# Dealing 32 weight-decode steps out anew among eight experts, with their raw words loaded one call earlier

## The chip, the cores and the metric

One core of one Trainium2 chip. The metric is the device time of one execution in microseconds (us). Engines: PE does matmuls (PEld loads its weights), DVE the vector work, ACT activations and copies, POOL index work and indirect DMAs, SP issues the other DMAs. Each engine works through its own queue in order.

## The reference

Three layers, each feeding the next. In float32:

```python
# 1. attention over 576 positions, 4 batches, 8 heads of 64; a causal window of 128; a bias per head
attn = softmax(where(mask, scale * q @ k.T + bias, -1e9)) ; x = attn @ v        # -> [2304, 512]
# 2. mixture of 8 experts: each token goes to the one with the largest logit
e = argmax(x @ w_gate); g = softmax(x @ w_gate)[e]
x = g * (relu(x @ w1[e]) @ w2[e])                                                # w1 [8,512,1024], w2 [8,1024,512]
# 3. one wide layer
out = relu(x @ w_in) ** 2 @ w_out                                                # w_in [512,2048], w_out [2048,512]
```

The weights of the third layer (w_in and w_out) arrive as 64-bit floats, so the kernel reads them as pairs of 32-bit words and makes 32-bit floats of them itself.

## The kernel before

Products are made from float16 pairs: a matrix is split into a high part (ACT: a cast with a scale) and a low part (DVE: what the cast left over), and three matmuls with float32 accumulation stand for one product. Only the first expert's product with w1 is done in float32.

**Order of the stages.** Attention comes first, and tokens are given to experts as it goes. The experts follow in an order found at run time (by how many tokens they have); the places in that order have fixed row counts (`ROWS`, 384 down to 224). Place e has two products: `s1` (8 column blocks `fc`, `h = relu(x w1)`; L790 to L792 on PE, L793 on ACT, L794 on DVE) and `s2` (4 blocks `d`; L844 to L846 on PE, a copy to `yT` on ACT, L847). While place e is computed, the weights of place e + 1 are brought in: after every second `fc` a quarter of w1, after every `d` a quarter of w2 (`load_w`). Each quarter is a DMA of 512 KB into a staging buffer (L742), split by ACT (L764) and DVE (L765) into a ring of 12 float16 tiles. The rest, tokens that found no room, is done under a branch (`overflow`, L1053) that is normally not taken, and the wide layer comes last (`moe2`).

**The decode steps.** The wide layer's weights must be ready, decoded and split, when that layer begins. This is cut into 32 steps that are strewn among the experts: 8 output steps (`out_step`, a block of w_out that is stored to DRAM again, `SENT`), 16 input steps (`in_step`, a piece of w_in, with four sums and differences of its blocks, since the wide input product has seven block products instead of eight, and hence seven operands), and 8 more output steps (`KEPT`). A step is: DMA of the raw words (one of 512 KB or two of 256 KB, L859), three word operations on DVE that make a float of a 64-bit pair (L864 to L866), for an input step four adds (L887 to L890), and a finish: the cast on ACT (L895 or L911) and the remainder on DVE (L896 or L912). All steps decode into one tile, `dec`.

**Where they are called.** `wide()` (L920) does one call: it finishes the step of the call before, then takes the next step, issues its DMAs and its decode. `STEPS` holds for each place at which `fc` of `s1` and after which `d` of `s2` a call stands. Counted from the code, calls lie thus: 6 ahead of place 0, then 2, 3, 2, 3, 3, 3, 3, 6 in the places 0 to 7, and 3 behind the branch. The seventh place (6) also starts the normalisation of the next layer.

**Buffers.** Raw words and weight quarters share four staging buffers (tag `rw`, bufs 4). Besides, the tiles `wi4` to `wi7`, which hold finished input weights later, serve as staging for part of the weights until they are needed: `SPARE` names which for each place, and `stage` (L748) takes them for every second quarter (every one for place 1).

**What sets the order.** The kernel is written for a framework that places the waits and decides each engine's order at build time: what stands earlier in the code goes first, but an instruction that is expected to be ready may go ahead of an earlier one that isn't. The order is fixed when the program runs.

Of the kernel before, what the change touches and what calls it, by code (L numbers as in the profile page):

```python
# [10 lines left out]
F32 = mybir.dt.float32  # L11
# [11 lines left out]
N, DM, E, F, F2 = 2304, 512, 8, 1024, 2048  # L23
# [22 lines left out]
TINY, HUGE = 1e-30, 1e30  # L46
GT = 2
GW = GT * P
STEPS = (((2, 6), ()), ((1, 5), (1,)), ((4,), (1,)), ((1, 5), (1,)), ((1, 5), (1,)), ((3,), (1, 3)), ((3,), (1, 3)),
         ((1, 3, 5, 7), (1, 3)))  # L50
SPARE = ((), (4, 5, 6, 7), (4, 5, 6, 7), (4, 5, 6, 7), (4, 5, 6, 7), (6, 7), (7,), ())
KEPT = (0, 1, 8, 9, 2, 3, 10, 11)
SENT = (4, 5, 12, 13, 6, 7, 14, 15)

# [35 lines left out]
class K:  # L90
# [656 lines left out]

    def stage(self, which, e, c):  # L748

        free = SPARE[e]  # L750
        n = 4 * (which - 1) + c
        if n % 2 == 0 and e > 1 or not free or (which, e) == (1, 1):
            return self.raw()
        return self.wi_s[free[(n if e == 1 else n // 2) % len(free)]].rearrange("p k a c -> p (k a c)").bitcast(F32)[:, :1024]

# [59 lines left out]
    def part(self, byte, n, dt=F32):  # L815
        t = self.work[:, byte // 4:byte // 4 + n * (2 if dt != F32 else 4) // 4]
        return t if dt == F32 else t.bitcast(dt)
# [33 lines left out]
    def wide_load(self, src, pieces):  # L851
        nc, V = self.nc, self.nc.vector
        n = sum(w for _, _, w, _ in pieces)
        wide = src.dtype != F32
        st = self.raw(U32 if wide else F32)[:, :1024 if wide else 512]
        for rows, c0, w, dst in pieces:
            r = src.bitcast(U32)[rows] if wide else src[rows]
            k = 2 if wide else 1
            nc.sync.dma_start(dst(st, k), c0(r, k))  # L859
        if not wide:  # L860
            return st
        t = self.dec[:, 512:] if len(pieces) > 1 else self.dec[:, :512]
        w = st.rearrange("p (n a) -> p n a", a=2)
        V.tensor_scalar(t, w[:, :, 1], 3, 0x3FFFFFFF, op0=ALU.logical_shift_left, op1=ALU.bitwise_and)  # L864
        V.scalar_tensor_tensor(t, w[:, :, 1], 0xC0000000, t, op0=ALU.bitwise_and, op1=ALU.bitwise_or)  # L865
        V.scalar_tensor_tensor(t, w[:, :, 0], 29, t, op0=ALU.logical_shift_right, op1=ALU.bitwise_or)  # L866
        return t.bitcast(F32)

    def in_step(self, fp, kp):

        nc, V = self.nc, self.nc.vector

        def part(j):
            blocks = slice(0, 4, 3) if j == 0 else slice(1, 3)
            return (slice((2 * j + kp) * P, (2 * j + kp + 1) * P),
                    lambda r, k: r.rearrange("p (i c) -> p i c", i=2)[:, :, k * fp * P:k * (fp + 1) * P],
                    2 * P,
                    lambda st, k: st.rearrange("p (b c) -> p b c", b=4)[:, blocks])

        f = self.wide_load(self.wi, [part(0), part(1)])  # L880
        d = self.dec.bitcast(F32).rearrange("p (b c) -> p b c", b=8)
        f4 = f.rearrange("p (b c) -> p b c", b=4)
        if self.wi.dtype == F32:
            nc.vector.tensor_copy(d[:, 4:], f4)
        a11, a12, a22, a21 = (d[:, 4 + b] for b in range(4))
        s1, s2, s3, s4 = (d[:, b] for b in range(4))
        V.tensor_tensor(s1, a21, a22, op=ALU.add)  # L887
        V.tensor_tensor(s3, a11, a21, op=ALU.subtract)
        V.tensor_tensor(s2, s1, a11, op=ALU.subtract)
        V.tensor_tensor(s4, a12, s2, op=ALU.subtract)  # L890
        src = self.dec.bitcast(F32)[:, :7 * P]
        dst = self.wi_s[fp]

        def finish():
            nc.scalar.activation(dst[:, kp, 0], src, AF.Copy, scale=WISC)  # L895
            nc.vector.scalar_tensor_tensor(dst[:, kp, 1], src, WISC, dst[:, kp, 0], op0=ALU.mult, op1=ALU.subtract)  # L896

        return finish

    def out_step(self, fc):  # L900

        nc = self.nc
        f = self.wide_load(self.wo, [(slice(fc * P, (fc + 1) * P), lambda r, k: r, DM, lambda st, k: st)])

        def finish():
            if fc in KEPT:
# [8 lines left out]
                self.stored.append(lambda: nc.sync.dma_start(self.wod[:, o:o + 2 * DM],  # L915
                                                             dst.rearrange("p a d -> p (a d)")))

        return finish

    def wide(self, k=1):  # L920
        def store():
            while len(self.stored) > (2 if self.steps and self.steps[0][0] != self.in_step else 0):
                self.stored.pop(0)()

        for _ in range(k):
            store()
            if self.finish:
                self.finish()
                self.finish = None
            if self.steps:  # L930
                f, *a = self.steps.pop(0)
                self.finish = f(*a)

    def open_wide(self, stack):
        wp = self.wp = stack.enter_context(self.tc.tile_pool(name="wp", bufs=1))
        self.wi_s = [wp.tile([P, 2, 2, 7 * P], F16, name=f"wi{k}", tag=f"wi{k}") for k in range(8)]
        self.wo_s = {}
        self.stored, self.finish = [], None
        self.steps = [(self.out_step, fc) for fc in SENT] + \
            [(self.in_step, fp, kp) for fp in range(8) for kp in range(2)] + [(self.out_step, fc) for fc in KEPT]  # L940

# [13 lines left out]
    def experts(self, stack):  # L955
# [35 lines left out]
        with tc.issue_after(self.last_gather.ins):  # L991
            for f in self.late:
                f()
        wide(2)
        self.s2([w[2, 0, k] for k in range(4)], self.hte, 0, EB * P, lambda d: wide())
        xt = self.new_xf(P)
        self.transpose_whole(xgs[0][0], xt)
# [226 lines left out]
    def moe2(self):  # L1224
# [9 lines left out]
        self.load_columns()  # L1234
        self.wide1(0, 1, first)
        self.turn_columns()
        while self.finish:
            self.wide()
        self.fetch_out()
        for G in range(NG):  # L1240
# [75 lines left out]
```

## Time and profile before

| | |
|---|---|
| median of three runs | 775.46 us (773.32, 775.46, 777.34) |
| profiled execution | 774.25 us, of which the span is 772.2 us |
| mean granted clock of TensorE | 0.984 of 2.4 GHz |
| busy share of the span | PE 94%, PEld 72%, DVE 70%, ACT 47%, POOL 17% |
| moved by DMA | 91.63 MB |

A profile shows one execution. The span runs from the first to the last instruction; what the execution takes beside it is outside the profile. The span is cut into stretches (windows), and for each the busy time of every engine is given, with the clock that TensorE was granted and the share in which the DMA engines were busy. An instruction's idle time before it is put down to what ended last among the things it waited for. An engine's queue is in order, so what waits at its head holds up all behind it.

In the profiled execution the experts begin at 179.93 us (first product of place 0) and the first matmuls of place 7 at 382.78; the branch is passed at about 415 us, and the wide layer takes the rest.

### The profile page before, as it was taken

To read this page: it belongs to the slowest core of one execution; us is meant where nothing else is said; L and a number is where in the kernel's file an instruction comes from. 1 tells how busy PE (TensorE), PEld (TensorE's weight loads), DVE (VectorE), ACT (ScalarE), POOL (GpSimd) and SP (SyncE) were. 2 spreads that over 40 slices of the span, in tenths; PEclk is the share of its full clock that TensorE was granted. 3 is DMA by queue.
4 is the path that set the end of the run, shared out by engine and by line. 5 is a ranking of instruction groups with operands and counts; after the bars stand their busy time and mean duration, and the time that the engine had idled before them with its cause. 6 is when DMAs were issued, how large, how long until landed. Compare 5 with 4: busy or idle time off the path is not lost. (4 is left out here: it accounts for less than half of the span.)

```text
span 772.2 us, 18404 instructions
## 1 busy us (share of the span) xinstructions
PE 728.1 (94%) x7547; PEld 559.2 (72%) x7547; DVE 540.1 (70%) x1352; ACT 361.2 (47%) x636; POOL 133.7 (17%) x183
## 2 busy tenths in 40 slices
PE   6989999998989899899798999999999999999996
PEld 5889899787646566688698777777777777777772
DVE  5898788855879897568798774747474756566440
ACT  5878898744556574465444342423232323323220
POOL 4583421525543020000000010101010000000001
PEclk9999999899999999999899999999999999999999
DMA  9796214867897874457514000000000000000000
GB/s 336 291 388 149 67 56 120 240 177 213 286 311 231 272 252 136 152 171 249 181 57 138 3 28 2 29 1 29 2 22 8 15 15 15 15 14 15 15 14 28
DMA packets 35650, 91.63 MB, mean 119 GB/s; under 512 B 5209, under 2 KB 13547, under 8 KB 35547
## 3 DMA queue, kind: packets, MB, share of 16 engines
q1 hardware_dynamic: 29803, 75.77, 30.3%
q0 software_dynamic: 5760, 14.65, 5.7%
q8 instruction: 61, 1.00, 0.5%
q14 instruction: 26, 0.21, 0.1%
HBM read 77.54 MB, written 13.04 MB: 117 GB/s over the span
## 5 line engine op out<-in xcount | busy, mean ns | idle before, releaser
L1159 PEld LDWEIGHTS <-wi 128*128 128x128 f16 x3024 | 170.4, 98 | 6.4 <-issue 2.6
L1220 POOL DMA_INDIRECT out_dram<-o,oid x18 | 17.5, 973 | 464.5 <-ACT o L1218 464.5
L1179 ACT CAST wr<-work 128x1024 f16<-128x1024 f32 x36 | 37.6, 1045 | 123.1 <-DVE work L1178 123.1
L845 PE MATMUL ps_c<-work,wr 128*128 128x352 f16 (+5 forms) x256 | 73.8, 294 | 10.2 <-DVE work L794 9.4
L844 PE MATMUL ps_c<-work,wr 128*128 128x352 f16 (+5 forms) x256 | 73.5, 293 | 5.9 <-ACT work L793 3.2
L846 PE MATMUL ps_c<-work,wr 128*128 128x352 f16 (+5 forms) x256 | 73.9, 294 | 0.0
L305 PE MATMUL ps_a<-yT,wr 128*128 128x192 f32 (+2 forms) x288 | 64.3, 343 | 6.6 <-DMA wr<-in_q_dram 5.0
L1184 DVE TENSOR_TENSOR work<-work 128x512 f32<-128x512 f32 x18 | 12.4, 692 | 77.2 <-ACT work L1171 77.2
L1159 PE MATMUL ps_c<-work,wi 128*128 128x128 f16 x1032 | 64.9, 219 | 0.0
L1159 PE MATMUL ps_a<-work,wi 128*128 128x128 f16 x1032 | 64.7, 219 | 0.0
L317 ACT ACTIVATE pb<-pb,nm 128x192 f32<-128x192 f32 (+2 forms) x144 | 56.2, 433 | 12.4 <-DVE nm L310 11.7
L1159 PE MATMUL ps_b<-work,wi 128*128 128x128 f16 x960 | 60.1, 219 | 1.5 <-DVEq L1057 1.5
L1211 PE MATMUL ps_d<-wr 128*128 128x512 f16 x144 | 54.6, 379 | 0.1
L1212 PE MATMUL ps_d<-wr 128*128 128x512 f16 x144 | 54.6, 379 | 0.0
L1213 PE MATMUL ps_d<-wr 128*128 128x512 f16 x144 | 54.6, 379 | 0.0
L1213 PE MATMUL ps_d<-rw,wr 128*128 128x512 f16 x144 | 54.6, 379 | 0.0
L1212 PE MATMUL ps_d<-rw,wr 128*128 128x512 f16 x144 | 54.6, 379 | 0.0
L1211 PE MATMUL ps_d<-rw,wr 128*128 128x512 f16 x144 | 54.6, 379 | 0.0
L1213 PEld LDWEIGHTS <-wr 128*128 128x128 f16 x288 | 28.1, 98 | 33.9
L765 DVE SCALAR_TENSOR_TENSOR wr<-rw,wr 128x1024 f16<-128x1024 f32 x36 | 43.7, 1217 | 11.1 <-ACT wr L764 11.0
L1180 DVE TENSOR_TENSOR wr<-work,wr 128x1024 f16<-128x1024 f32 x36 | 44.0, 1221 | 10.0 <-ACT wr L1179 10.0
L305 PEld LDWEIGHTS ps_a<-yT,wr 128*128 128x128 f32 x288 | 45.1, 199 | 7.8 <-DMA yT<-in_k_dram 6.1
(248 smaller groups left out, 1693.8 us busy)
## 6 DMA issues: line engine op xcount, KB each, us to landing
rw<-in_w_dram SPq DMA_DIRECT2D x36, 512.0 KB, 5.5
wi<-in_w_dram SPq DMA_DIRECT2D x24, 512.0 KB, 5.3
rw<-in_wo_dram SPq DMA_DIRECT2D x16, 512.0 KB, 4.2
rw<-in_wi_dram SPq DMA_DIRECT2D x32, 256.0 KB, 5.2
wr<-in_q_dram SPq DMA_DIRECT2D x14, 512.0 KB, 8.0
xd<-xhl POOLq DMA_DIRECT2D x16, 256.0 KB, 4.5
yT<-in_k_dram SPq DMA_DIRECT2D x7, 576.0 KB, 10.7
rw<-in_v_dram SPq DMA_DIRECT2D x12, 325.0 KB, 5.6
```

The costliest lines, as they stand in the source:

```text
L305: nc.tensor.matmul(ps[:, s, first:hi], q[g, u, hh // 4][:, hh % 4, s if u < 4 else 0, :], self.kt[g, hh // 2][:, hh % 2, key0:key0 + hi - ...
L317: self.last_exp = nc.scalar.activation(pb[:, s, first:hi], pb[:, s, first:hi], AF.Exp, bias=nm[:, s:s + 1], scale=-1.0)
L765: self.nc.vector.scalar_tensor_tensor(t[:, 1], st, sc, t[:, 0], op0=ALU.mult, op1=ALU.subtract)
L844: nc.tensor.matmul(py, wh, hh, start=fc == 0, stop=False)
L845: nc.tensor.matmul(py, wh, hl, start=False, stop=False)
L846: self.last_mm = nc.tensor.matmul(py, wl, hh, start=False, stop=fc == 7)
L1159: self.nc.tensor.matmul(ps[:, j], w[:, kp, a, w0 * P:(w0 + 1) * P], v[:, 2 * x + kp], start=kp + b == 0, stop=kp == 1 and b == 2)
L1179: nc.scalar.copy(g[0][:, :, i], ci)
L1180: V.tensor_tensor(g[1][:, :, i], ci, g[0][:, :, i], op=ALU.subtract)
L1211: nc.tensor.matmul(py, gh, wh, start=n == 0, stop=False)
L1212: nc.tensor.matmul(py, gh, wl, start=False, stop=False)
L1213: nc.tensor.matmul(py, gl, wh, start=False, stop=n == 15)
```

## The change

`STEPS` deals the calls out anew: 7 ahead of place 0, then 3, 4, 3, 4, 3, 1, 0, 6 in the places 0 to 7, and 3 behind the branch. A step is now a generator with three parts, and each call of `wide()` begins one step and moves every begun step on by one part, the oldest first: so a call finishes the step begun two calls earlier, decodes the one begun in the call before, and issues the DMAs of a new one. `SPARE` goes; `stage` counts how many input steps have begun and offers as staging those of `wi4` to `wi7` whose own step is at least two steps off, for every second quarter as before (from place 2 on). In `moe2` the loop that drains the steps asks for `begun`.

```diff
--- before.py
+++ after.py
@@ -46,9 +46,8 @@
 TINY, HUGE = 1e-30, 1e30
 GT = 2
 GW = GT * P
-STEPS = (((2, 6), ()), ((1, 5), (1,)), ((4,), (1,)), ((1, 5), (1,)), ((1, 5), (1,)), ((3,), (1, 3)), ((3,), (1, 3)),
+STEPS = (((1, 4, 6), ()), ((1, 5), (0, 2)), ((5,), (0, 2)), ((1, 5), (0, 2)), ((3,), (0, 2)), ((), (1,)), ((), ()),
          ((1, 3, 5, 7), (1, 3)))
-SPARE = ((), (4, 5, 6, 7), (4, 5, 6, 7), (4, 5, 6, 7), (4, 5, 6, 7), (6, 7), (7,), ())
 KEPT = (0, 1, 8, 9, 2, 3, 10, 11)
 SENT = (4, 5, 12, 13, 6, 7, 14, 15)
 
@@ -747,9 +746,10 @@
 
     def stage(self, which, e, c):
 
-        free = SPARE[e]
+        begun = 16 - sum(f == self.in_step for f, *_ in self.steps) if e > 0 and (which, e) != (1, 1) else 16
+        free = [k for k in range(4, 8) if begun + 2 <= 2 * k]
         n = 4 * (which - 1) + c
-        if n % 2 == 0 and e > 1 or not free or (which, e) == (1, 1):
+        if n % 2 == 0 and e > 1 or not free:
             return self.raw()
         return self.wi_s[free[(n if e == 1 else n // 2) % len(free)]].rearrange("p k a c -> p (k a c)").bitcast(F32)[:, :1024]
 
@@ -857,7 +857,11 @@
             r = src.bitcast(U32)[rows] if wide else src[rows]
             k = 2 if wide else 1
             nc.sync.dma_start(dst(st, k), c0(r, k))
-        if not wide:
+        return st
+
+    def wide_words(self, st, pieces):
+        nc, V = self.nc, self.nc.vector
+        if st.dtype == F32:
             return st
         t = self.dec[:, 512:] if len(pieces) > 1 else self.dec[:, :512]
         w = st.rearrange("p (n a) -> p n a", a=2)
@@ -877,7 +881,10 @@
                     2 * P,
                     lambda st, k: st.rearrange("p (b c) -> p b c", b=4)[:, blocks])
 
-        f = self.wide_load(self.wi, [part(0), part(1)])
+        pieces = [part(0), part(1)]
+        st = self.wide_load(self.wi, pieces)
+        yield
+        f = self.wide_words(st, pieces)
         d = self.dec.bitcast(F32).rearrange("p (b c) -> p b c", b=8)
         f4 = f.rearrange("p (b c) -> p b c", b=4)
         if self.wi.dtype == F32:
@@ -895,12 +902,16 @@
             nc.scalar.activation(dst[:, kp, 0], src, AF.Copy, scale=WISC)
             nc.vector.scalar_tensor_tensor(dst[:, kp, 1], src, WISC, dst[:, kp, 0], op0=ALU.mult, op1=ALU.subtract)
 
-        return finish
+        yield
+        finish()
 
     def out_step(self, fc):
 
         nc = self.nc
-        f = self.wide_load(self.wo, [(slice(fc * P, (fc + 1) * P), lambda r, k: r, DM, lambda st, k: st)])
+        pieces = [(slice(fc * P, (fc + 1) * P), lambda r, k: r, DM, lambda st, k: st)]
+        st = self.wide_load(self.wo, pieces)
+        yield
+        f = self.wide_words(st, pieces)
 
         def finish():
             if fc in KEPT:
@@ -915,7 +926,8 @@
                 self.stored.append(lambda: nc.sync.dma_start(self.wod[:, o:o + 2 * DM],
                                                              dst.rearrange("p a d -> p (a d)")))
 
-        return finish
+        yield
+        finish()
 
     def wide(self, k=1):
         def store():
@@ -924,18 +936,18 @@
 
         for _ in range(k):
             store()
-            if self.finish:
-                self.finish()
-                self.finish = None
             if self.steps:
                 f, *a = self.steps.pop(0)
-                self.finish = f(*a)
+                self.begun.append(f(*a))
+            for i, step in enumerate(list(self.begun)):
+                if next(step, True):
+                    self.begun.remove(step)
 
     def open_wide(self, stack):
         wp = self.wp = stack.enter_context(self.tc.tile_pool(name="wp", bufs=1))
         self.wi_s = [wp.tile([P, 2, 2, 7 * P], F16, name=f"wi{k}", tag=f"wi{k}") for k in range(8)]
         self.wo_s = {}
-        self.stored, self.finish = [], None
+        self.stored, self.begun = [], []
         self.steps = [(self.out_step, fc) for fc in SENT] + \
             [(self.in_step, fp, kp) for fp in range(8) for kp in range(2)] + [(self.out_step, fc) for fc in KEPT]
 
@@ -991,7 +1003,7 @@
         with tc.issue_after(self.last_gather.ins):
             for f in self.late:
                 f()
-        wide(2)
+        wide(3)
         self.s2([w[2, 0, k] for k in range(4)], self.hte, 0, EB * P, lambda d: wide())
         xt = self.new_xf(P)
         self.transpose_whole(xgs[0][0], xt)
@@ -1234,7 +1246,7 @@
         self.load_columns()
         self.wide1(0, 1, first)
         self.turn_columns()
-        while self.finish:
+        while self.begun:
             self.wide()
         self.fetch_out()
         for G in range(NG):
```

## Rows read from the trace of the kernel before

**Rows 1.** Windows, e0 to e6: length; PE, PEld, DVE, ACT, POOL busy; clock, DMA
```profile
179.93:198.92 18.99, 14.30 (x179) 13.68 (x177) 13.82 (x26) 10.55 (x21) 7.30 (x15) 1.00 0.84 256
198.92:235.98 37.06, 34.60 (x220) 20.56 (x217) 29.90 (x50) 20.10 (x31) 17.09 (x23) 0.95 0.88 296
235.98:268.38 32.40, 30.36 (x218) 19.97 (x216) 30.06 (x67) 18.37 (x27) 8.04 (x7) 1.00 0.78 254
268.38:299.23 30.85, 30.26 (x218) 19.81 (x216) 27.96 (x49) 19.28 (x30) 4.35 (x3) 1.00 0.75 237
299.23:331.80 32.57, 28.09 (x211) 20.45 (x209) 20.59 (x33) 16.45 (x26) 0.00 (x0) 0.95 0.35 114
331.80:354.77 22.97, 22.13 (x211) 19.64 (x208) 18.45 (x32) 13.82 (x23) 0.00 (x0) 1.00 0.77 249
354.77:382.78 28.01, 23.10 (x197) 18.68 (x195) 21.73 (x41) 14.92 (x24) 0.00 (x0) 0.88 0.60 191
```

**Rows 2.** Windows, one us in e6, PE alone: length, busy, granted clock, DMA
```profile
377.00:378.00 1.00, 1.00 (x7) 0.50 1.05 336
```

**Rows 3.** Timeline of DVE in e4: start, us, instruction, [idle before, its releaser]
```profile
300.73 0.43 DVE L864 TENSOR_SCALAR dec<-rw 128x512 uint32<-128x512 uint32 x1 [1.95 <-DMA rw<-in_wi_dram]
306.26 1.22 DVE L765 SCALAR_TENSOR_TENSOR wr<-wi,wr 128x1024 f16<-128x1024 f32 x1
307.40 0.46 DVE L794 SCALAR_TENSOR_TENSOR work<-ps_a,work 128x304 f16<-128x304 f32 x1
315.55 0.43 DVE L864 TENSOR_SCALAR dec<-rw 128x512 uint32<-128x512 uint32 x1 [2.16 <-DMA rw<-in_wi_dram]
```

**Rows 4.** Timeline of PE in e4 and in e6
```profile
307.92 0.29 PE L790 MATMUL ps_a<-work,wr 128*128 128x304 f16 x1 [1.88 <-DVE work L794]
372.25 0.27 PE L844 MATMUL ps_c<-work,wr 128*128 128x256 f16 x1 [2.08 <-ACT work L793]
```

**Rows 5.** Timeline of ACT in e6
```profile
370.18 1.06 ACT L764 ACTIVATE wr<-rw 128x1024 f16<-128x1024 f32 x1 [2.21 <-DMA rw<-in_w_dram]
371.82 0.39 ACT L793 ACTIVATE work<-ps_a 128x256 f16<-128x256 f32 x1
```

**Rows 6.** Lines view: busy us, mean ns, idle before
```profile
L864 DVE TENSOR_SCALAR dec<-rw 128x512 uint32<-128x512 uint32 x32 | 13.6, 424 | 15.9 <-PE ps_c L846 7.9 <-DMA rw<-in_wi_dram 5.3 <-DMA rw<-in_wo_dram 2.2
L865 DVE SCALAR_TENSOR_TENSOR dec<-rw,dec 128x512 uint32<-128x512 uint32 x32 | 22.1, 689 | 0.5
L887 DVE TENSOR_TENSOR dec<-dec 128x128 f32<-128x128 f32 x16 | 4.6, 287 | 0.3
L896 DVE SCALAR_TENSOR_TENSOR wi<-dec,wi 128x896 f16<-128x896 f32 x16 | 17.4, 1086 | 7.8 <-ACT wi L895 7.8
```

**Rows 7.** Windows, L864 alone: length, busy us (count)
```profile
170.00:299.23 129.23, 7.62 (x18) 0.99 0.79 256
299.23:382.78 83.55, 2.98 (x7) 0.94 0.55 177
```

**Rows 8.** Waits of the DMA queue, 170 to 425 us: total, times, longest
```profile
SPq L742 <- DVE wr L765: 43.3, 13, 8.7
```

**Rows 9.** The page's part 6: issues, KB each, median us to landing
```profile
rw<-in_w_dram SPq DMA_DIRECT2D x36, 512.0 KB, 5.5
```

**Rows 10.** Timeline of DVE and PE behind the overflow branch
```profile
418.92 0.43 DVE L864 TENSOR_SCALAR dec<-rw 128x512 uint32<-128x512 uint32 x1 [2.17 <-DMA rw<-in_wo_dram]
422.54 0.67 DVE L912 SCALAR_TENSOR_TENSOR wr<-dec,wr 128x512 f16<-128x512 f32 x1
423.46 0.22 PE L1122 MATMUL ps_b<-sd,onesb 128*128 128x128 bf16 x1 [0.79 <-DVE sd L1117]
430.87 0.38 PE L1211 MATMUL ps_d<-wr 128*128 128x512 f16 x1
```

**Rows 11.** Line view of L865 in e1 and in e4: min/median/max ns
```profile
L865 DVE SCALAR_TENSOR_TENSOR dec<-rw,dec x6: 682/685/693, 201.1 to 231.1; 128x512 uint32<-128x512 uint32 x6
L865 DVE SCALAR_TENSOR_TENSOR dec<-rw,dec x2: 691/692/693, 301.2 to 316.0; 128x512 uint32<-128x512 uint32 x2
```

## Prediction

> **What bounds the kernel now.** I read the stretches of the eight experts first: cut the span where the first matmuls of an expert's first product start and compare length, PE busy and granted clock [rows 1]. I call the experts by their place in the order, e0 to e7; the seventh is e6. Where PE busy equals the length PE is the bound, and the rest is what can be won. Idle PE (length less busy): e0 4.69 us, e1 2.46, e2 2.04, e3 0.59, e4 4.48, e5 0.84, e6 4.91. To this comes the slow clock: after such a gap PE runs for a while at 0.50, that is 1.2 of 2.4 GHz [rows 2]. A stretch with mean clock c loses about (1 - c) x busy: e1 0.05 x 34.60 = 1.7, e4 0.05 x 28.09 = 1.4, e6 0.12 x 23.10 = 2.8. So e4 costs 5.9, e6 7.7, e1 4.2, e0 4.7, and all of e0 to e6 about 26 us. Everything else in them is PE at full rate, which the change doesn't touch.
>
> Then why the gaps are there. DVE is the second engine: it is busy 29.90 of 37.06 us in e1, 30.06 of 32.40 in e2, 27.96 of 30.85 in e3, but 20.59 of 32.57 in e4 and 21.73 of 28.01 in e6 [rows 1]. In e4 the gaps are not DVE work but DVE waiting in its queue: L864, the first word operation of a decode, stood at the head for 1.95 and 2.16 us until its raw words landed; the weight splits (L765, 1.22 us) and L794, which PE needs, lay behind it [rows 3]. PE's gap of 1.88 us ends with exactly that L794 [rows 4]. In e6 it is ACT: L764, a weight split, waited 2.21 us for its words with L793 behind it [rows 5], and PE's gap of 2.08 ends with L793 [rows 4].
>
> **The change, part by part.** It adds and removes no arithmetic. It moves 32 steps, splits each into three calls (load, decode, finish) where there were two (load with decode, finish), and makes the place of weight words depend on how many steps have begun.
>
> *Cost of a step.* An input step on DVE: L864 0.424, L865 0.689, L866 like it, four adds of 0.287, L896 1.086 [rows 6]: 4.0 us; an output step has neither adds nor L896 but an L912, put at the length of L866, so 2.5 us.
>
> *Dealing out.* By the code 16 decodes lay before the end of e3, then 3 each in e4, e5, e6. The trace has one decode ahead of e0 and 18 in all up to the end of e3, then 7 up to the end of e6 [rows 7]: instructions are not run in strict order of the code, decodes run ahead when DVE has room. By the new code 20 decodes lie before the end of e3, 3 in e4, 1 in e5, none in e6. So against the trace at least 2 steps, 8 us of DVE, enter e0 to e3, and e6 loses its 3 decodes and finishes, about 10 us of its 21.73.
>
> *e4.* Both waits at L864 go, if the words of a step are asked for one call earlier; three calls in 32.57 us lie some 10 us apart, and the whole wait was 1.95 and 2.16. Bounds: nothing gained (the load waits for a buffer just as long), or all 5.9. What is late next is the splitting itself, as in e3 and e5, which lose 0.59 and 0.84. I take 0.8 left: -5.1.
>
> *e6.* With half of DVE's work gone and no word loads between the weight loads, bounds are 0 and -7.7. I take the rest that e2 shows, 2.0, since weights stay late (below): -5.7. e5: nothing, it has 0.84.
>
> *e0 to e3.* The cover for the 8 us is DVE's idle time, 5.17 + 7.16 + 2.34 + 2.89 = 17.6 us [rows 1]. Part of that is waiting for ACT between the two halves of a finish, which every further step has too. Bounds: 0, or all 8 us late for PE; below 0 too, by up to the 11.5 that these stretches lose, if words that are there earlier close gaps, for which I see no wait at L864 in these rows. The nearest row is e2, where DVE is 93% busy and PE still loses only 2.04. With e1 and e3 as full as e2, e3 goes from 0.59 to 2.0 and e1 and e2 lose some 0.8 each: +3.0. The loads ahead are SP's: four more DMAs of 256 KB, two steps' words, in stretches whose DMA share is 0.84 and 0.88; at e1's 296 GB/s they take 3.5 us, and e1 has 12% of 37 us, 4.4 us, free. SP issues them ahead of weight loads, which are needed only half an expert later. That is why I don't charge them again.
>
> *Buffers.* Words loaded ahead hold one of the four raw buffers from a load to the next call, all through e6 too. And the weights of places 5 and 6 lose their spare buffers (wi6, wi7): by the new rule there are none once 13 input steps have begun, which is before e4. In e6 the load count hardly differs: 11 loads over 4 buffers before (2.75 each), 8 over 3 now (2.67). In e4 and e5 it was (4 + 3) / 4 = 1.75 and becomes 2.67. SP already waits 43.3 us in weight loads for L765 to free a buffer [rows 8]. A buffer's turn is 5.5 us to landing [rows 9], 1.06 on ACT [rows 5], 1.22 on DVE [rows 3]: 7.8 us, so eight loads over three buffers take 20.8 us. PE at full clock needs 28.09 - 1.4 = 26.7 us in e4, 22.13 in e5, 20.3 in e6 [rows 1]. It just fits, with half an expert of slack before a weight is needed. Bounds: 0, and in each of e4 and e5 what e6 loses today. Nearest to 0; I take +1.5.
>
> *Behind the experts.* At 418.92 L864 waits 2.17 us for the last step's words, which SP could only ask for after the overflow branch; PE then waits 0.79 for L1117, queued behind [rows 10]. Now the second-last step is decoded there and its words were asked for before the branch. The gap goes, -0.8. In exchange one more decode and finish (2.5 us) lies in that full stretch of DVE; the last finish (L912, today at 422.54), then some 2 to 5 us later, feeds a matmul at 430.87 [rows 10]. Bounds -0.8 and +3; I take -0.5.
>
> **A rule against it.** POOL is busy 17.09 us in e1 and not at all in e4 [rows 1], and the change moves decodes from the latter side to the former. L865, with two inputs in SBUF, takes 685 ns (median) in e1 and 692 in e4 [rows 11]: no price. The Trainium skill, SBUF — State Buffer, section "Who interferes with whom", holds that a DVE instruction with two SBUF inputs and a GpSimd instruction that reads SBUF lock each other out for a whole instruction. By that rule the trace should have shown it, and it doesn't. As a mechanism of this kernel: two steps have 14 such instructions, a POOL instruction in e1 lasts 17.09 / 23 = 0.74 us, so at most 10 us of DVE and on average (46% busy, half an instruction) 2.4. That is a rival below.
>
> **Sum.** -5.1 - 5.7 + 3.0 + 1.5 - 0.5 = -6.8 us. Against the profiled execution (774.25 us, of which 772.2 are span) that is 767.5. The median of the runs lies 1.2 above the profiled one, so 768.7 us.
>
> **Rivals.** *Given back:* the gaps of e4 and e6 close, but e0 to e3 pay 6 us and the buffers 4: -5.1 - 5.7 + 6 + 4 - 0.5 = -1.3, so 774. For it: DVE is at 93% in e2 already; the steps run by readiness, so that little may move at all (the change not doing what it says gives 775.5). Against: 17.6 us of idle DVE. *POOL's lock* (by that rule): +2.4 to +10 on DVE; at a middle of 5 us all late for PE 773.7, no change. *Slower:* the raw buffers decide. From the point at which weights come late in two of e4, e5, e6 as they do once today, ACT's queue stands at L764 with L793 behind it, and each costs 7.7: 2 x 7.7 + 0.8 = 16.2 against 5.9 + 0.8 + 7.7 = 14.4 today, +1.8, +3 in e0 to e3, -0.5: +4.3, so 779.8. For it: 20.8 us for eight loads against 20.3 in e6, and the lost spare buffers. Against: slack of half an expert. *Better:* nothing is paid: -5.1 - 6.9 (0.8 left in e6) - 0.8 = -12.8, so 762.7.
>
> **How the numbers follow.** A measurement of this kernel can tell about 0.5% from no change, here 3.9 us: faster is below 771.6, slower above 779.3. Chances: my forecast (765 to 771.6) 0.40, better 0.13, given back 0.23, POOL's lock 0.02, slower rival 0.22; of this last 0.04 stays within 0.5% and 0.18 lies above 779.3 (with weights late in all three experts it is 3 x 7.7 against 14.4, so 787). Faster 0.53, same 0.29, slower 0.18. The likeliest case's own range is 765 to 771.6; for 8 in 10 I go from 762 to 780, which leaves out some 0.04 below and 0.16 above.
>
> **What would show it.** Right: no wait at L864 for raw words in e4 and none at about 419; e4 near 27.5 us, e6 near 22.5 to 23.5 with clock 1.00; DVE in e6 near 11 us; e1 to e3 longer by 1 us each at most. Wrong: e1 to e3 together longer by over 5 us with DVE full (given back); ACT L764 waiting for weight words before gaps of PE in e4 to e6 (slower); L865 longer than 0.7 us in e1 (lock); as many decodes up to the end of e3 as today (nothing moved).

## The result: 0.9% slower, and the profile after

The changed kernel takes 781.96 us (median of 15 runs, 778.70 to 786.34), the kernel before 775.86 (15 runs): the ratio of the means of these runs is 1.0089, 95% interval 1.0069 to 1.011 (6.9 us; the medians are 0.8% apart). I had forecast 768.7 in a range of 762 to 780. The profiled execution took 783.05 us, 781.3 of them span, 9.1 more than the 772.2 before.

The stretches of the eight experts after, cut as in [rows 1]: length; PE, PEld, DVE, ACT, POOL busy; clock, DMA.

```profile
182.90:200.43 17.53, 14.29 (x180) 13.69 (x178) 13.05 (x24) 10.89 (x22) 7.36 (x14) 1.00 0.88 278
200.43:239.14 38.71, 34.93 (x220) 20.55 (x218) 30.80 (x52) 17.95 (x28) 21.92 (x28) 0.96 0.84 262
239.14:278.05 38.91, 33.60 (x217) 21.18 (x216) 32.06 (x68) 20.51 (x30) 4.32 (x4) 0.91 0.68 216
278.05:313.50 35.45, 31.97 (x218) 20.37 (x216) 29.87 (x56) 20.04 (x29) 2.89 (x3) 0.95 0.67 206
313.50:342.23 28.73, 26.59 (x210) 19.69 (x208) 23.56 (x42) 15.68 (x25) 0.00 (x0) 1.00 0.62 186
342.23:370.61 28.38, 24.01 (x211) 20.57 (x208) 20.88 (x34) 16.91 (x26) 0.00 (x0) 0.94 0.72 227
370.61:390.05 19.44, 19.44 (x196) 17.54 (x194) 12.72 (x21) 12.23 (x21) 0.00 (x0) 1.00 0.65 218
```

Against [rows 1]: e6 is 8.6 us shorter, with PE busy all the time, and e4 3.8 shorter. But e1 to e3 take 113.07 us where they took 100.31, 12.8 more, and e5 takes 5.4 more. What lies ahead of e0 is 3.0 us longer, e0 1.5 shorter, e7 0.5 and the rest 1.3 longer: 9.1 in all. Two of these numbers say little about the change. e0 starts at 179.58, 181.49 and 181.86 us in three kernels tried below (runs 3, 9 and 13) whose work up to there is the same, so the 3.0 us ahead of it lie mostly within what one profile differs from the next. And the 1.3 us at the end are a slow clock: in the 4.3 us from 423.23 on TensorE was granted 0.54 and then 0.65 of its full clock, and 1.00 in the corresponding stretch before.

Of the 12.8 us, idle PE makes 7.5 (12.6 for 5.1) and the slow clock behind the gaps, by (1 - clock) x busy, some 4.3 (6.0 for 1.7). DVE is busy 92.7 us in e1 to e3, only 4.8 more, and its share falls (82% in e2, which had 93%), and so does that of the DMA engines (0.68 for 0.78). No engine became full there; something came late.

What came late are the weights. ACT's waits for them from e1 to e6, before and after (total, times, longest):

```profile
ACT wr L764 <- DMA rw<-in_w_dram: 15.5, 10, 3.3
ACT wr L764 <- DMA wi<-in_w_dram: 8.0, 6, 2.1
```

```profile
ACT wr L764 <- DMA rw<-in_w_dram: 39.8, 21, 5.0
ACT wr L764 <- DMA wi<-in_w_dram: 6.6, 4, 3.1
```

23.5 us became 46.4. How that reaches PE is seen in e2 and e5, in the timelines of PE, ACT and DVE of the changed kernel (start, us, instruction, [idle before, releaser]):

```profile
264.78 0.31 PE L844 MATMUL ps_c<-work,wr 128*128 128x352 f16 x1 [1.84 <-ACT work L793]
351.04 0.27 PE L790 MATMUL ps_a<-work,wr 128*128 128x256 f16 x1 [2.95 <-DVE work L794]
...
263.32 1.06 ACT L764 ACTIVATE wr<-rw 128x1024 f16<-128x1024 f32 x1 [5.03 <-DMA rw<-in_w_dram]
264.29 0.45 ACT L793 ACTIVATE work<-ps_b 128x352 f16<-128x352 f32 x1
...
348.17 2.48 DVE L765 SCALAR_TENSOR_TENSOR wr<-rw,wr 128x1024 f16<-128x1024 f32 x2 [0.86 <-ACT wr L764]
350.57 0.42 DVE L794 SCALAR_TENSOR_TENSOR work<-ps_a,work 128x256 f16<-128x256 f32 x1
```

At 263.32 ACT's split had stood 5.03 us at the head of the queue with L793 behind it, which PE needed: the pattern of [rows 5], now in e2. At 348.17 two splits of late weights lie ahead of the L794 that ends PE's gap.

Why the weights are late is seen in SP's queue. First its order at the start of e1, before and then after:

```profile
199.27 0.33 SPq L859 DMA_DIRECT2D rw<-in_wo_dram  x1
200.66 0.33 SPq L915 DMA_DIRECT2D wod<-wi  x1
202.59 0.34 SPq L742 DMA_DIRECT2D rw<-in_w_dram  x1
```

```profile
201.20 0.33 SPq L859 DMA_DIRECT2D rw<-in_wo_dram  x1
202.59 0.33 SPq L926 DMA_DIRECT2D wod<-wi  x1
204.51 1.30 SPq L859 DMA_DIRECT2D rw<-in_wi_dram  x2
205.95 0.50 SPq L926 DMA_DIRECT2D wod<-wi  x1
208.20 1.20 SPq L859 DMA_DIRECT2D rw<-in_wi_dram  x2
212.40 0.33 SPq L926 DMA_DIRECT2D wod<-wi  x1
213.93 0.36 SPq L741 DMA_DIRECT2D rw<-in_w_dram  x1
```

One word load stood ahead of e1's first weight load, now three do: it goes out 13.5 us behind the start of e1 instead of 3.7, and the eighth still goes out 34.8 us behind it instead of 23.6. Not only words stand ahead of it: the stores of finished output blocks (`wod`, L926) are three where there was one. Of the time up to it SP waited 6.2 us before word loads and 4.4 before stores, these mostly (3.9) for a decode's finish on DVE (L923). Then what SP's weight loads waited for from e1 to e6 (total, times, longest), before and after, a selection of each:

```profile
SPq L742 <- DVE wr L765: 43.3, 13, 8.7
...
SPq L742 <- DVE dec L887: 6.7, 4, 3.9
SPq L742 <- DVE dec L866: 5.1, 4, 1.9
```

```profile
SPq L741 <- DVE wr L765: 28.9, 12, 4.2
SPq L741 <- DVE dec L870: 15.6, 5, 6.2
SPq L741 <- DVE dec L868: 10.9, 3, 4.6
SPq L741 <- DVE dec L894: 9.4, 6, 4.8
SPq L741 <- DVE dec L897: 3.9, 3, 2.0
```

Weight loads that waited until a decode was done (all releasers that write `dec`) come to 12.6 us before and to 40.0 after, each with one line of under 1 us that isn't shown. A raw buffer with words in it comes free only when DVE has decoded them, and the weight load that needs it can't go out. But this number tells who holds the weight loads, not how long they are held: their waits for all releasers together come to 84.3 us before and to 88.5 after. What grew is the time by which the weights are late for ACT. The weights that now pass through these buffers are 45 quarters; they were 36 [rows 9].

The rows on the steps themselves, after: the first word operation (L868 now) in two windows as in [rows 7], its last wait with the one of PE behind the branch as in [rows 10], and L869 in e1 and in e4 as in [rows 11].

```profile
170.00:313.50 143.50, 8.46 (x20) 0.95 0.73 228
313.50:390.05 76.55, 2.10 (x5) 0.98 0.66 209
...
426.95 0.43 DVE L868 TENSOR_SCALAR dec<-rw 128x512 uint32<-128x512 uint32 x1 [2.61 <-DMA rw<-in_wo_dram]
432.57 0.22 PE L1134 MATMUL ps_b<-sd,onesb 128*128 128x128 bf16 x1 [0.49 <-DVE sd L1129]
...
L869 DVE SCALAR_TENSOR_TENSOR dec<-rw,dec x7: 681/693/693, 203.1 to 237.5; 128x512 uint32<-128x512 uint32 x7
L869 DVE SCALAR_TENSOR_TENSOR dec<-rw,dec x4: 692/693/693, 313.5 to 340.0; 128x512 uint32<-128x512 uint32 x4
```

As forecast, 20 decodes lie up to the end of e3 (18 before); e4 to e6 have 5 (7 before, and 4 by my count). By stage, e1, e2 and e3 have 7, 4 and 5 where they had 6, 4 and 4. So e2, which grew most (6.5 us), has no more decodes than before.

### The profile page after: what moved, and what is told of

Read it like the earlier page. It is cut to its first block, busy times and chain, and to the rows that moved or that the text cites. A ratio compares the mean times of both kernels' runs of the same rounds, so it can differ in the third digit from the quotient of the medians.

```text
span 781.3 us, 18406 instructions
## 1 busy us (share of the span) xinstructions
PE 733.6 (94%) x7547; PEld 563.2 (72%) x7547; DVE 538.8 (69%) x1352; ACT 361.6 (46%) x636; POOL 135.0 (17%) x183
## 5 line engine op out<-in xcount | busy, mean ns | idle before, releaser
L845 PE MATMUL ps_c<-work,wr 128*128 128x352 f16 (+5 forms) x256 | 73.1, 291 | 9.6 <-DVE work L794 7.9
L844 PE MATMUL ps_c<-work,wr 128*128 128x352 f16 (+5 forms) x256 | 72.8, 291 | 5.1 <-ACT work L793 3.6
L846 PE MATMUL ps_c<-work,wr 128*128 128x352 f16 (+5 forms) x256 | 73.1, 291 | 0.0
L304 PE MATMUL ps_a<-yT,wr 128*128 128x192 f32 (+2 forms) x288 | 66.3, 351 | 6.6 <-DMA wr<-in_q_dram 4.7
L764 ACT ACTIVATE wr<-rw 128x1024 f16<-128x1024 f32 x45 | 47.3, 1058 | 40.2 <-DMA rw<-in_w_dram 39.8
L765 DVE SCALAR_TENSOR_TENSOR wr<-rw,wr 128x1024 f16<-128x1024 f32 x45 | 54.8, 1222 | 15.8 <-ACT wr L764 15.2
```

The source lines that it names most:

```text
L304: nc.tensor.matmul(ps[:, s, first:hi], q[g, u, hh // 4][:, hh % 4, s if u < 4 else 0, :], self.kt[g, hh // 2][:, hh % 2, key0:key0 + hi - ...
L764: self.nc.scalar.activation(t[:, 0], st, AF.Copy, scale=sc)
L765: self.nc.vector.scalar_tensor_tensor(t[:, 1], st, sc, t[:, 0], op0=ALU.mult, op1=ALU.subtract)
L844: nc.tensor.matmul(py, wh, hh, start=fc == 0, stop=False)
L845: nc.tensor.matmul(py, wh, hl, start=False, stop=False)
L846: self.last_mm = nc.tensor.matmul(py, wl, hh, start=False, stop=fc == 7)
```

## The experiments

The runs are called by their numbers, run 1 to run 18; e0 to e7 are the experts. The expectations weigh two theories: by theory B (buffers; with it goes the order in SP's queue) words that hold a raw buffer make the weights late, by theory D (DVE) the steps dealt into e1 to e3 make DVE too full there.

Ratios are to the kernel before, run beside each, with 95% intervals; 0.1% is 0.8 us. A stage length of one profile is uncertain by more than the ratios: e1 took 37.25, 36.72 and 39.24 us in three kernels (runs 3, 7 and 11) whose work up to there is the same.

**Each half alone.** Run 2 keeps the new dealing and loads in the same call as it decodes; run 3 loads a call ahead with the old dealing and the old spare buffers.

```diff
 run 2, in in_step and out_step:
         st = self.wide_load(self.wi, pieces)
-        yield
         f = self.wide_words(st, pieces)
 run 3: STEPS, SPARE, stage and wide(2) as in the kernel before, the rest as changed
```

> The changed kernel with the load of a step back in the call of its decode: only the new dealing and the new rule for spare buffers are left. Theory B: no buffer is held between calls, so e2 and e3 lose most of their excess over before (6.5 and 4.6 us); e4 gets its waits at the decode back, 2 to 4 us; time 770 to 776. Theory D: as slow as the changed kernel, 779 to 784.

> The kernel before with its own dealing and its own spare buffers; only the load goes one call ahead. Theory B: weights late and L793 behind L764 in e1 to e3 as in the changed kernel, the time 778 to 784. Theory D: no more DVE work in e1 to e3 than before, so 772 to 777, or less where the wait for raw words at the decode goes.

Run 2: 1.0072 (1.0046 to 1.0098). Run 3: 0.9969 (0.9944 to 0.9994). Both came out as theory D said. The loss is the dealing's. Loading ahead is no cost by itself, rather a gain of some 2 us, but it doesn't lessen the dealing's price. In run 2 the first weight load of e1 also goes out behind three word loads, 11.4 us behind the start of e1, e1 to e3 take 110.9 us, and ACT waits as long for weights from e1 to e6 (50.4 us with a second line of 7.6):

```profile
ACT wr L764 <- DMA rw<-in_w_dram: 42.8, 20, 5.3
```

Its weight loads wait 26.3 us for decodes, against 40.0. So words that are held from one call to the next are not needed for the loss.

**Another dealing.** Run 8 leaves e6 empty too, but deals its steps into e4 and e5 instead of e0 to e3; run 11 has 6 calls ahead and leaves one step in e6; run 12 has 6 ahead and a third call in e0.

```diff
-STEPS = (((1, 4, 6), ()), ((1, 5), (0, 2)), ((5,), (0, 2)), ((1, 5), (0, 2)), ((3,), (0, 2)), ((), (1,)), ((), ()),
+STEPS = (((2, 6), ()), ((1, 5), (1,)), ((4,), (1,)), ((1, 5), (1,)), ((1, 3, 5), (1,)), ((1, 5), (1, 3)), ((), ()),
 run 11: the same with ((3,), ()) for e6 and wide(2) ahead; run 12: with ((1, 4, 6), ()) for e0 and wide(2) ahead
```

> The changed kernel with another dealing: 7 calls ahead of e0 and none in e6 as in the changed kernel, but 2, 3, 2, 3 in e0 to e3 as before and 4 and 4 in e4 and e5. DVE or queue theory (the cost is that more steps stand in e1 to e3): e1 to e3 return to 100-102 us together (113 in the changed kernel), e6 stays near 19.5, e4 and e5 take some 55 to 57, and the time is 766-770, below both kernels. Spare theory: e5 and e6 stay as slow as in the changed kernel or get slower, 774-780.

> The changed kernel with another dealing: 6 calls ahead of e0 as before (the run with 7 had three word loads in the way of e1's first weight load and an e1 of 40.7 us), 2, 3, 2, 3 in e0 to e3, 4, 4 and 1 in e4 to e6. If the seventh call ahead was what made e1 long: e1 near 37.3, e1 to e3 101-102 us, e6 below 21 us, time 765-769, below both kernels. If e1 stays near 40: 769-772.

> The same with no call in e6 and a third call in e0 (6 ahead, then 3, 3, 2, 3, 4, 4, 0). If a step more ahead of or in e0 is what makes e1 late, e1 is near 40 us as in the run with 7 ahead and the time is 768-772; if not, e1 is near 37.3 and the time is 764-768.

Run 8: 0.997 (0.9942 to 0.9997), run 11: 0.996 (0.9935 to 0.9984), run 12: 0.9957 (0.9929 to 0.9985). The windows of e1, e2, e3 and e6 in run 8:

```profile
198.71:239.45 40.74, 35.60 (x220) 20.83 (x217) 31.61 (x52) 21.11 (x31) 19.14 (x26) 0.92 0.85 276
239.45:274.04 34.59, 31.48 (x218) 20.44 (x216) 29.78 (x66) 18.71 (x28) 3.49 (x3) 0.95 0.73 235
274.04:303.98 29.94, 29.94 (x218) 19.86 (x216) 27.53 (x50) 18.86 (x28) 4.15 (x3) 1.00 0.72 236
359.36:378.81 19.45, 19.45 (x197) 17.55 (x195) 12.59 (x21) 12.10 (x21) 0.00 (x0) 1.00 0.72 236
```

In the code only the dealing differs between the changed kernel and run 8 (the staging rule follows it: 41 quarters pass through the raw buffers instead of 45). It is worth 1.2%, some 9 us, and e1 to e3 come to 105.3 us instead of 113.1, while e6 keeps its whole gain. So the steps moved into e0 to e3 are what cost. Run 8 still missed its expectation (e1 to e3 at 100 to 102 us): with e6 empty, e4 and e5 together are at 55.4, no longer than before but 2.6 above run 3's 52.8. That e1's length came from the seventh call ahead is not borne out: it was 39.24 and 38.82 in runs 11 and 12, which have six, and both came out as the second or slower branch of their expectation. Against run 3 (0.9969), which loads ahead with the old dealing, none of the three gains much more than 0.1%, less than the intervals can tell. So what they gain on the kernel before is what loading ahead gains; that a better dealing adds to it is not shown.

**DVE work or word loads, added.** To the kernel of run 3: in run 9 the first sum of a step made again, in run 10 an additional load, in run 13 both, in each of the experts e1 to e3.

```diff
                 if d in STEPS[e][1]:
                     wide()
+                if 1 <= e <= 3 and d in (1, 3):      runs 9, 13: 4 or 10 more adds, dec <- dec
+                    self.again(4 if d == 1 else 10)
+                if 1 <= e <= 3 and d == 3:           runs 10, 13: one more load of 512 KB of words
+                    self.more_words()
```

> The kernel that loads a call ahead and deals the steps out as before (772.98 us), with 14 more adds of 128x128 (0.287 us each, the first sum of the step just decoded, made again) in each of e1, e2 and e3: 4 behind the second block of the second product and 10 behind its last, 4.0 us an expert, as much DVE time as one more step, 12 us in all; no more words, no buffers. DVE theory (e1 to e3 got longer since DVE had more steps to do there): e1 to e3 grow from 101.7 to 108-113 us, the time to 779-784. Buffer and queue theory (it was the additional word loads): e1 to e3 grow by 0 to 3 us, the time is 773-776.

> The counterpart: the same kernel without the adds, but with one more load of a step's raw words (two DMAs of 256 KB into a raw buffer) behind the last block of the second product in each of e1, e2 and e3; the buffer is held until the next call, where DVE reads one column of it. 0 DVE time to speak of. Buffer and queue theory: weight loads go out later, ACT waits more at L764, e1 to e3 grow by 4 to 10 us, the time is 777-783. DVE theory: e1 to e3 grow by less than 2 us, 773-775.

> The kernel that loads a call ahead with the old dealing (ratio 0.9969 to the kernel before), with both additions of the two runs before: 4.0 us of adds on DVE and one more load of raw words in each of e1, e2, e3. If the two costs add up (0.66% and 0.34%): ratio 1.006 to 1.008, e1 to e3 near 109 us. If they do more together (late words and a full DVE queue hold each other up): 1.010 or more, e1 to e3 112 us or more. If the one hides in the other: 1.003 to 1.005.

Run 9: 1.0035 (1.0013 to 1.0056), run 10: 1.0003 (0.9973 to 1.0032), run 13: 1.0044 (1.0024 to 1.0065). So 12 us of DVE work cost 0.66% (5 us, uncertain by 2.5), three loads 0.34% with an uncertainty of 0.4%, and both 0.75%: no more than their sum, and by the expectation's ranges less, though the interval reaches the sum. Run 9 fell between its two expectations (e1 to e3 take 105.0 us); run 10 has the time of one theory and the 105.8 us in e1 to e3 of the other. The DVE work shows itself as late weights too; ACT's waits of run 9, to be read against 15.7 and 12.4 us in run 3:

```profile
ACT wr L764 <- DMA rw<-in_w_dram: 26.4, 15, 4.1
ACT wr L764 <- DMA wi<-in_w_dram: 7.8, 8, 1.7
```

**DVE work or word loads, taken out** of the changed kernel, for the three steps begun behind the third block of the second product in e1 to e3.

```diff
 run 14:
         st = self.wide_load(self.wi, pieces)
         yield
+        if odd:
+            V.tensor_copy(self.junk, st[:, :1])
+            yield
+            nc.gpsimd.memset(self.wi_s[fp][:, kp], 0.0)
+            return
 run 15: wide_load is left out, and the word operations read dec in place of st
```

> The changed kernel in which three of the steps begun in e1 to e3 (those behind the third block of the second product) load their words and hold the buffer until the next call, but are not decoded or split (their part of w_in is set to zero on POOL); DVE has 12 us less to do there. DVE theory: most of the loss comes back, ratio 0.998 to 1.002, e1 to e3 104 us or less. Buffer and queue theory: ratio 1.006 to 1.009, e1 to e3 110 us or more. By the run with more DVE work (0.66% for 12 us): 1.002 to 1.004.

> The counterpart: the same three steps load no words; all their DVE and ACT work is done, on what lies in the tile that the decodes write to, so that these three blocks of w_in are not what they should be. Three loads of 512 KB and their buffer turns less in e1 to e3. Buffer and queue theory: ratio 0.998 to 1.002, e1 to e3 104 us or less. DVE theory: 1.006 to 1.009, 110 us or more. By the run with more words (0.34% for three): 1.005 to 1.007.

Run 14: 1.0009 (0.9989 to 1.003), 0.8% or 6 us below the changed kernel. Run 15: 1.0047 (1.0025 to 1.0068), 0.4% or 3 us below. The sizes are those of the additions, each uncertain by 0.3%. But the place of run 14's gain is not the one I expected: e1 to e3 stay at 113.7 us, as the other theory had it, with 15 decodes where 16 were (one of the three would by the code have been decoded in e4, and later steps are decoded in the room); the time is won in e4 and e5, 50.3 us for 57.1:

```profile
312.20:340.43 28.23, 26.17 (x211) 19.67 (x208) 21.87 (x34) 17.85 (x28) 0.00 (x0) 1.00 0.63 200
340.43:362.48 22.05, 22.01 (x210) 19.67 (x208) 13.27 (x20) 13.30 (x22) 0.00 (x0) 1.00 0.62 216
```

**A shorter decode, in both kernels.** Runs 4 and 18 leave two of the three word operations out, 32 x 2 x 0.689 = 44 us of DVE [rows 6].

```diff
-        V.scalar_tensor_tensor(t, w[:, :, 1], 0xC0000000, t, op0=ALU.bitwise_and, op1=ALU.bitwise_or)
-        V.scalar_tensor_tensor(t, w[:, :, 0], 29, t, op0=ALU.logical_shift_right, op1=ALU.bitwise_or)
```

> The changed kernel without two of the three word operations of each decode (the floats are then wrong): DVE has 1.4 us less per step, some 27 us less up to the end of e3, while loads, buffers and their order of use stay. Theory D: e1 to e3 fall to the lengths of before or less, time at most 772. Theory B: L764 still waits over 35 us for weight words, e2 stays above 36 us, time 776 to 781.

> The kernel before with two of the three word operations left out in every decode (so that the third layer's weights are not what they should be); the same cut took the changed kernel from 1.0089 to 0.9817, 2.7%. DVE theory (the change lost by DVE work in e1 to e3, of which the cut takes some 1.4 us a step): the kernel before gains less than the changed one, 0.985 to 0.990, since its steps lie where DVE has room, so that the two kernels come out within 0.5% of each other. If DVE had nothing to do with the loss: it gains the same 2.7%, 0.971 to 0.975, and the distance of 0.9% stays.

Run 4: 0.9817 (0.9785 to 0.9849), run 18: 0.9862 (0.9826 to 0.9897). The cut gives the changed kernel 2.7% and the kernel before 1.4%. One us of DVE work costs 21.1 / 44 = 0.48 us in the one and 10.7 / 44 = 0.24 in the other; by run 9 it is 5.1 / 12 = 0.43 and by run 14 6.2 / 12 = 0.51. With short decodes the change wouldn't lose, as theory D said of run 18. But this doesn't part DVE's work from the late weights: in run 4 the first weight load of e1 goes out 1.0 us behind the start of e1 instead of 13.5, and ACT waits 20.2 us for weights instead of 46.4, and what stands ahead of that load waits for decodes, which are shorter there. And e1 to e3 still take 107.0 us there, against 99.7 in run 18.

**The buffers.** Run 1 has five raw buffers in the changed kernel, run 17 in the kernel before, run 16 in the kernel of run 11; to make room for the fifth, the ring of gather tiles is cut from six to four. Run 6 is the changed kernel with that cut alone. Run 7 is run 3 without the spare staging for the weights of places 4 to 6, so that 48 quarters pass through the four buffers.

```diff
-        self.rw = ctx.enter_context(tc.tile_pool(name="rw", bufs=4))
+        self.rw = ctx.enter_context(tc.tile_pool(name="rw", bufs=5))
 tag "xg", three places:
-bufs=6
+bufs=4
 run 7:
-SPARE = ((), (4, 5, 6, 7), (4, 5, 6, 7), (4, 5, 6, 7), (4, 5, 6, 7), (6, 7), (7,), ())
+SPARE = ((), (4, 5, 6, 7), (4, 5, 6, 7), (4, 5, 6, 7), (), (), (), ())
```

> The changed kernel with a fifth raw buffer (room for it from the pool xg, 4 tiles in place of 6; the experts use three at a time). Theory B (the raw buffers: the words loaded ahead hold one, weights come late, the weight split L764 stands at the head of ACT's queue with L793 behind it): the waits of L764 for weight words, 46 us from e1 to e6 in the changed kernel, fall below 25, e2 to at most 35 us, e3 to 32, e5 to 25, and the time to 766 to 772. Theory D (DVE is too full in e1 to e3 with the steps dealt to them): e1 to e3 stay within 2 us of the changed kernel, e5 alone may gain, time 776 to 782.

> The changed kernel with four instead of six gather tiles and the four raw buffers that it has. It is the control of the run with five raw buffers, which had this shorter gather ring too and in which PE stood 7.49 us in e1 for a gather. If that pause is the shorter ring's price, this kernel is at 785-789 and the fifth raw buffer by itself is worth 7 to 11 us (buffer theory: all of what the change lost); if the ring costs nothing, it is at 781-783 and the fifth buffer is worth only 4 us.

> The kernel that loads a call ahead but deals the steps out as before (772.98 us), with the spare staging of the places 4 to 6 taken away, so that all weight quarters of e5 to e7 go through the four raw buffers, as they do in the changed kernel. Spare theory (the lost spare buffers make the weights late): e4 to e6 grow, L764 waits there for weights, 776-780. Queue or DVE theory (what costs is in e1 to e3): 772-774.

> The dealing with one step in e6 (ratio 0.996) with five raw buffers and a gather ring of four. If raw buffers bound the milder dealing too, as the fifth was worth some 0.5% in the changed kernel: ratio 0.991 to 0.994, 768 us. If they were short only because of the additional steps in e1 to e3: 0.995 to 0.998.

> The kernel before with five raw buffers and a gather ring of four. The fifth buffer was worth some 0.5% in the changed kernel and 0.6% in the one with one step in e6. If raw buffers bound the kernel before too: ratio 0.993 to 0.996, and the shortage of buffers is common to all and not what the change lost by. If they became short only by the change (buffer theory of the loss): 0.998 to 1.001.

Run 1: 1.005 (1.0029 to 1.0071), run 6: 1.0099 (1.0061 to 1.0136), run 7: 1.0001 (0.9973 to 1.003), run 16: 0.9897 (0.9865 to 0.9929), run 17: 0.9996 (0.9969 to 1.0024). The fifth buffer is worth 0.5% in the changed kernel (run 1 against run 6) and 0.6% in the milder dealing (run 16 against run 11), each uncertain by 0.4%; the shorter ring by itself costs 0.1% (run 6 against the changed kernel), with the same uncertainty. Run 1's time is that of theory D, not the 766 to 772 of theory B, and ACT's waits fall to 32.1 us, not below 25: the buffers are a part of the loss, not the whole of it. In run 17 a fifth buffer doesn't show, but this doesn't say that the buffers don't bound the kernel before: there, as in run 16, PE pays for the shorter ring in the expert e1, while e2 runs without a gap. The gather pause in run 17 (it is 5.28 us in run 16 and 4.63 in run 6):

```profile
221.14 0.82 PE L781 MATMUL ps_d<-id,xg 96*128 96x96 f16 x8 [6.24 <-DMA xg<-xd,idx]
```

The windows of e1, e2 and e3 in run 16:

```profile
197.03:239.02 41.99, 35.43 (x220) 20.96 (x217) 33.28 (x55) 22.92 (x33) 17.59 (x24) 0.92 0.85 286
239.02:268.89 29.87, 29.87 (x217) 20.02 (x216) 27.43 (x62) 16.37 (x26) 5.17 (x5) 1.00 0.73 242
268.89:298.84 29.95, 29.95 (x219) 19.86 (x216) 27.37 (x49) 18.13 (x28) 4.48 (x3) 1.00 0.69 221
```

Run 7 cost 0.3% against run 3, less than the two intervals can tell apart. Run 16, loading ahead with a milder dealing and a fifth buffer, is the version that beats both: 765.4 us, 1.0% below the kernel before. Its weight loads wait 37.0 us for decodes, nearly as long as the changed kernel's 40.0, but ACT waits only 20.0 us for weights: of the two numbers the second goes with the time here, though not in every kernel (run 3, with 28.1 us, is faster than the kernel before, with 23.5). Run 3 with a fifth buffer, which would tell what the dealing adds here, was not tried.

**The words in POOL's queue.** Run 5 asks for the words on POOL, so that they are out of SP's way.

```diff
-            nc.sync.dma_start(dst(st, k), c0(r, k))
+            nc.gpsimd.dma_start(dst(st, k), c0(r, k))
```

> The changed kernel, with the raw words of the steps asked for from POOL's queue instead of SP's; buffers, dealing and all DVE work stay. Queue theory (in e1 the word loads stand ahead of the weight loads in SP's in-order queue and wait there for a raw buffer, so that the first weight load of e1 went out at 213.93 us where it was 202.59 before; the late weights then stop ACT and DVE): the weight loads of e1 go out some 10 us earlier, ACT waits at L764 for weights well under 46 us, the time falls by 4 to 8 us to 774-778. Buffer theory (a weight load finds its buffer held by words, whoever asks): the weight loads of e1 stay late and the time stays at 780-784. DVE theory (too much DVE work in e1 to e3): no change either, 780-784. Against a gain: POOL is busy 21.92 us in e1 and its own waits would delay gathers.

1.0499 (1.0443 to 1.0556), 811 us, which neither theory expected. The words' issue at 217.12 stood in POOL's queue behind gathers and index work that fill it from 205.06 on. The issue on POOL, DVE's wait for it and PE's gap in e1:

```profile
217.12 1.42 POOL L859 DMA_DIRECT2D rw<-in_wi_dram  x2
221.43 0.43 DVE L868 TENSOR_SCALAR dec<-rw 128x512 uint32<-128x512 uint32 x1 [14.54 <-DMA rw<-in_wi_dram]
222.37 0.48 PE L790 MATMUL ps_a<-work,wr 128*128 128x384 f16 x1 [14.20 <-DVE work L794]
```

So the run moves the same kind of wait to another queue and doesn't tell the price of SP's order apart. Nor did SP's queue get free: the first weight load of e1 went out at 224.70, 29.4 us behind the start of e1, behind three stores that waited 28.5 us for the finishes of decodes (L923). What the run shows is how much a late step costs when DVE's queue stands on it.

## Why the prediction was wrong

- *e6, -5.7:* -8.6. Right in kind and too small: with no steps left no gap remains, not even the 2.0 us that I kept.
- *e4, -5.1:* -3.8. No wait at L868 is left in it; 2.1 us of idle PE remain instead of 0.8.
- *e0 to e3, +3.0:* +11.3 (-1.5 in e0, +12.8 in e1 to e3). This is the step that failed. The decodes moved as counted, and their work on DVE was not badly priced: 8 us at the 0.43 to 0.51 us per us of runs 9 and 14 are some 4. What failed is the sentence that SP issues the loads ahead of weight loads "which are needed only half an expert later. That is why I don't charge them again". The slack was not there: in e1 the weight loads went out 10 us later, behind words and behind stores that I hadn't counted at all, and ACT's waits for weights in e1 to e3 rose from 11.4 to 32.1 us. I also took DVE's idle time as cover. Part of it was DVE waiting for ACT's splits of weights (2.5 us before, 6.4 after, at L765), and work put there delays the stores, the buffers' return and with them the loads.
- *Buffers, +1.5 in e4 and e5:* e5 alone is 5.4 us longer, and the longest gap in it (2.95) ends behind two splits of late weights. "Half an expert of slack" was an argument from rates, 20.8 us for eight loads; it left out that word loads share the buffers and stay in them for a whole call. In run 2, where they don't stay, e5 takes 23.1 us, but e4, with its waits at the decode back, 34.1. The fifth buffer gave 0.5% back, uncertain by 0.4%.
- *Behind the experts, -0.5:* +1.8 with e7, of which 1.3 are the slow clock behind the branch. L868 still waits there, 2.61 us at 426.95: the last step's words are asked for behind the branch as before. PE's wait is 0.49 instead of 0.79.
- *POOL's lock:* L869 takes 693 ns in e1 with POOL busy 21.92 us, and 693 in e4 with POOL idle. No lock shows, as I took it. But this trace hardly tries the rule: of POOL's instructions in e1 only six, 4.2 us, are arithmetic on the indices (L990), the rest are issues of DMAs, and my estimate had counted all of POOL's instructions alike.
- *Given back* had the right sign of each term, but its mark, DVE full, is not what the profile shows: DVE's share fell. *Slower* had the right mechanism, ACT at L764 with L793 behind it and the raw buffers deciding, and nearly the right time (779.8), but put it into e4 to e6; it came first in e1 to e3. I gave it 0.22.

What stays open: e1 to e5 are 15.7 us longer than in run 3's kernel, by one profile of each. Two more decodes' DVE work (some 4), three more loads (2.6, uncertain by 3) and the lost spare buffers (run 7, 2.5, uncertain by 3) make some 9 when added one at a time. That the rest comes from where the loads stand, three steps' words and their stores ahead of e1's first weight load, was read from SP's queue and not tried by itself. The runs agree with it: this load goes out 2.5 to 3.7 us behind the start of e1 in the kernels with one step's words ahead of it (before, runs 3, 7, 9, 10, 11, 13), whose e1 to e3 take 100 to 106 us; 7.6 and 8.0 us behind it with two (runs 8 and 12: 105 and 108 us); 11 to 14 us behind it with three (the changed kernel, runs 2, 6, 14, 15: 110 to 114 us). Run 4 doesn't fit (1.0 us, and 107), nor quite does run 1 (7.2 us, and 111, of which 7.5 are a pause of PE for a gather). And these kernels differ in their steps too, so that this is agreement and no proof.

## What to carry to other kernels

A piece of work that is moved takes along its buffer and its place in each in-order queue: before counting an engine's idle time as cover, list what will stand ahead of the next loads in the DMA queue, and afterwards sum how long the consumer waits for its data, not only whom the loads wait for. Idle time of an engine that waits for late data is no room; here each us of DVE work that was added or taken out cost 0.24 us in the kernel before and 0.43 to 0.51 in the others, although DVE was idle 12% of e1 to e3 before the change and 18% after it. And a dealing that empties the stage with the worst gap is only worth what the stage that receives the work doesn't lose: dealt into e4 and e5 it gained nothing that can be told from loading ahead alone, dealt into e0 to e3 it lost.
